# Global filter and MoE on one core: x's first rows through SyncE, a new order of the first batch, Strassen in two chunks more

## The chip, the cores and the metric

The kernel runs on one core of a Trainium2 chip. The metric is device time in microseconds for one launch. Before the change the median of seven runs is 757.11 us (755.1 to 759.68).

The core's engines are TensorE (PE, with PEld for its weight loads), VectorE (DVE), ScalarE (ACT), GpSimd (POOL) and SyncE (SP). In this kernel transfers are issued from SP (queue q1, "hardware dynamic") and from POOL (queue q0, "software dynamic"); only POOL's transfers change fp32 to fp16 on the way.

## What is computed

```python
def _attn_ref(x, filt_r, filt_i):            # x: 8 x 3008 x 256
    X = np.fft.rfft(x, axis=1)
    F = (filt_r + 1j * filt_i)[None, :, :]
    Y = X * F
    y = np.fft.irfft(Y, n=x.shape[1], axis=1)
    return y.astype(np.float32)

def _moe_ref(x, w_in, w_out):                # x: 24064 x 256
    h = x @ w_in                             # 256 x 2048
    g = np.maximum(0.01 * h, h)
    return (g @ w_out).astype(np.float32)    # 2048 x 256
```

The result of the first goes, as 24064 tokens of 256 numbers, into the second.

## The kernel before, in words

**The transform.** A sequence of 3008 is treated as 94 x 32. Stage 1 (s1) is a matrix product over the 94 (`fwd1`), stage 2 (s2) one over the 32 with the twiddle factors in it (`f2`), then comes the product with the filter, then stage 3 (sa, the inverse over 32) and stage 4 (sb, the inverse over 94, matrix `i1`). Between stages 1 and 2, and between 3 and 4, the data must be turned. Stage 4 leaves a batch transposed in `yt`, from which the MoE reads.

**The MoE.** The 24064 tokens form 47 chunks of 512. For each, `moe1` makes h in pairs of 128 rows of w_in (line 501) and ACT turns a pair into g (line 506, leaky ReLU). The second product of a chunk runs while the next chunk's first product does, interleaved matmul by matmul. It is made either in `plain` (line 607: 64 matmuls of 256 columns) or in `products` (line 555): Strassen's scheme in Winograd's form, seven products of 16 matmuls with 128 columns each, over the four quarters of g and of w_out. That needs four sums of quarters of g per chunk (`act_sums`, line 529, VectorE), four sums of w_out once (line 635), and adds that put the products together (lines 579 to 599). The seventh product of a chunk (`last_product`) is made in the slot of the next chunk. Chunks from `W0 = 4` on run so, except the last; chunks 0 to 3 and 46 run in `plain`.

**The first batch.** It is not planned by times but by a list written out by hand, `FIRST`, in which each step is one instruction or a few: s1p (stage 1 on PE), s1e (its copy out of PSUM, A on ACT or D on DVE), t1 (turning, a transpose on VectorE), s2p (stage 2 on PE), s2d (filter product on VectorE from PSUM), s2a and s2m (copy by ACT and filter product on GpSimd), sap and sae (stage 3 and its copy), t2 (second turning), sbp and sbe (stage 4 and its copy), warm (matmuls on zeros), i1 and x (loads of the inverse matrix and of the second batch's x, the latter with w_out between its halves). The engines take their parts of the list in its order. A load whose place must be kept back, such as i1, begins with a small memset on VectorE on the destination, for which the load waits.

Ahead of the list stand the loads: SP issues `small` (fwd1 and the stage 3 matrices) and two thirds of f2; POOL issues x of batch 0 in four parts of 10, 10, 8 and 4 rows, four filter loads, the last third of f2, four filter loads, and w_in. A POOL transfer waits for the eighth before it (the semaphores go round in eight).

**The other batches** are planned by time. The unit is an eighth of a chunk. `PLANS` gives for batches 1 to 3, and for all later ones with a shift of 47 units per batch, where stage 1 begins and its step, the same for stage 2, by how much stage 3 lies behind, begin and step of stage 4, and the place of the x loads of the next batch. Groups are taken one by one, at least `GAP` = 0.6 units apart. The data are turned through DRAM: SP stores stage 1's (line 254) `AFTER[0]` behind the last group, and reads them back (line 261) `LANDED` behind that; stage 3's (lines 324, 268) likewise with `AFTER[4]`. A group of stage 2 or 4 is taken at or behind its read-back's time. In stage 2 the product with the filter needs the two halves of the partitions exchanged: VectorE makes two products (lines 307, 310), SP copies one with its halves exchanged (lines 308, 309) `AFTER[1]` behind, and GpSimd adds (line 313) `AFTER[2]` behind (batch 1: `AFTER[3]`); stage 3 (line 320) needs that sum. Even groups of batch 1 exchange on VectorE (lines 304, 305).

Of the kernel before, what the change touches and what calls it, by code (L numbers as in the profile page):

```python
# [11 lines left out]
P = 128  # L12
# [63 lines left out]
def kernel(  # L76
# [21 lines left out]
    QT = 4 * N1  # L98
    W0 = 4
    GAP = 0.6  # L100
    EXG = 0
    LANDED = 2.25
    SUMS = (0.13, 1.43, 2.87, 3.89)
    REST = (5.89, 12.39, 11.94, 9.93, 24.7, 19.52)
    DUE = (3.46, 1.74)
    TWICE = (1.43, 1.46)
    F2T = 2.82
    LEAD = (3.88, 5.77)
    AFTER = (0.67, 0.83, 2.35, 2.75, 0.3, 0.45)


    PLANS = (
        (0.68, 0.07, 11.58, 1.13, 3.65, 36.62, 2.68, 5.42, 1.67),
        (11.38, 1.67, 43.14, 2.5, 7.25, 86.56, 2.69, 18, 2.16),
        (39.96, 1.81, 76.39, 3.57, 5.42, 129.9, 2.68, -0.73, 2.69),
        (63.95, 2.85, 119.86, 3.87, 7, 177.42, 2.97, 12.93, 2.45),
    )
# [84 lines left out]


    nc.sync.dma_start(small_sb[:], small_d.ap())
    for i in (1, 0):
        nc.sync.dma_start(f2_sb[:, ts(i, NC // FP), :], f2_d.ap()[i])
    first_parts = ((0, 10), (10, 10), (20, 8), (28, 4))
    for n0, nn in first_parts:
        x_load(0, n0, nn)
    for hf in range(2):  # L210

        filt_load(0, filt_r, hf * DH, DH)
        filt_load(64, filt_i, hf * DH, DH)
        if hf == 0:
            nc.gpsimd.dma_start(f2_sb[:, ts(2, NC // FP), :], f2_d.ap()[2])
    nc.gpsimd.dma_start(w_in_sb[:], moe_w_in.rearrange("(dt p) c -> p dt c", p=P))
# [232 lines left out]

    def load_x():  # L450

        x_load(1, 0, N2 // 2)
        nc.gpsimd.dma_start(w_out_sb[:], moe_w_out.rearrange("(ct p) d -> p ct d", p=P))
        x_load(1, N2 // 2, N2 // 2)
        issued.add(("x", 1, 0))

    FIRST = """
        warm 18, s1p 0 0 2 b0, s1e 0 0 2 A, s1p 0 2 4 b3, s1p 0 6 4 b4, s1e 0 2 4 D, warm 4, s1p 0 16 4 b3,
        s1e 0 16 4 D, s1p 0 10 2 b1, s1e 0 6 4 A, s1p 0 12 4 b4, s1e 0 10 2 A, warm 2, s1p 0 24 2 b2,
        s1e 0 12 4 A, s1e 0 24 2 D, s1p 0 20 4 b3, s1e 0 20 4 A, s1p 0 26 2 b0, s1p 0 28 2 b1,  # L460
        s1p 0 30 2 b2, s1e 0 26 2 D, s1e 0 28 2 A, s1e 0 30 2 D, t1 1, t1 0, warm 14, s2p 0 0 4 0 b0,
        s2p 0 0 4 1 b1, s2p 0 16 4 0 b2, t1 2, t1 3, s2a 0 0 4 0, s2m 0 0 4 0, s2a 0 0 4 1, s2p 0 16 4 1 b0,
        s2p 0 8 8 0 b4, s2p 0 8 8 1 b3, s2a 0 16 4 0, s2m 0 16 4 0, s2a 0 16 4 1, s2m 0 16 4 1,
        s2p 0 4 4 0 b1, s2d 0 8 8 0, s2p 0 20 4 1 b2, s2d 0 8 8 1, i1, s2d 0 4 4 0, s2p 0 4 4 1 b0,
        s2p 1 8 8 0 b4, s2d 0 4 4 1, warm 1, s2p 1 8 8 1 b3, s2a 1 8 8 0, s2m 0 0 4 1, sap 0 8 b1,
        s2a 1 12 8 0, s2p 1 16 8 0 b4, s2d 0 20 4 1, sap 0 16 b0, s2m 1 12 8 0, x, s2a 1 8 8 1, s2m 1 8 8 1,
        s2d 1 16 8 0, sae 0 8 A, s2a 1 12 8 1, sae 0 16 A, s2p 0 20 4 0 b2, sap 0 4 b1, s2m 1 12 8 1,
        s2p 1 16 8 1 b3, sap 0 0 b0, s2p 1 0 8 1 b4, s2d 0 20 4 0, s2d 1 16 8 1, sae 0 4 A, s2m 1 8 8 0,
        sae 0 0 A, sap 0 20 b1, s2d 1 0 8 1, sap 0 12 b2, s2p 1 0 8 0 b3, sap 1 16 b0, sae 0 20 A,
        sae 0 12 A, sap 1 12 b1, s2d 1 0 8 0, sap 1 20 b2, t2 0, sap 1 8 b4, t2 1, sae 1 16 A, sap 1 4 b0,  # L470
        sap 1 0 b3, sae 1 12 A, warm 5, sbp 0 1 b1, sae 1 20 A, sae 1 8 A, sbp 0 4 b2, sae 1 4 A, sae 1 0 A,
        t2 3, sbp 0 5 b4, sbe 0 1 A, sbp 0 2 b0, t2 2, sbe 0 4 A, sbp 0 6 b3, sbe 0 5 A, sbp 0 7 b1,
        sbp 0 0 b2, sbp 0 3 b4, sbe 0 6 A, sbp 1 1 b3, sbe 0 0 D, sbe 0 2 A, sbp 1 0 b0, sbe 0 3 A,
        sbe 0 7 A, sbe 1 1 D, sbe 1 0 A
    """
    steps = dict(s1p=s1p, s1e=s1e, t1=t1, s2p=s2p, s2d=s2d, s2a=s2a, s2m=s2m, sap=sap, sae=sae, t2=t2,
                 sbp=sbp, sbe=sbe, i1=load_i1, x=load_x, warm=keep_warm)
    for step in FIRST.split(","):
# [12 lines left out]
    def moe1(ci, ct):  # L491
# [13 lines left out]
        if j == 1:  # L505
# [10 lines left out]
    sums = big[0][:, : 3 * NCH * TH].rearrange("p (i c t) -> p i c t", i=3, c=NCH)  # L516
    s1, s2, s4 = (sums[:, i] for i in range(3))
    part = [big[0][:, 3 * NCH * TH :].bitcast(FP32)[:, ts(i, 2 * TH)].rearrange("p (t k d) -> p t k d", t=2, k=2)
            for i in range(2)]
# [4 lines left out]

    def act_sums(ci, step):
        a11, a12, a21, a22 = (quarter(ci, i, j) for i in range(2) for j in range(2))
        o, i0, i1, op = ((s1, a21, a22, AL.add), (a21, a11, a21, AL.subtract),
                         (s2, s1, a11, AL.subtract), (s4, a12, s2, AL.subtract))[step]
        nc.vector.tensor_tensor(o, i0, i1, op)  # L529
        issued.add(("sum", ci, step))  # L530

    done = {"products": 0}

    def store(ci, tj, of):

        t, end = ci * CH + tj * P, ci * CH + (tj + 1) * P
        lo = 0
        while t < end:
            e = min(end, (t // QT + 1) * QT)
            b, h = divmod(t // QT, N2 // 4)  # L540
            row = b * N + (t % QT) // 4 * N2 + 4 * h
            nc.sync.dma_start(
                bass.AP(tensor=out.tensor, offset=out.offset + row * D,
                        ap=[[N2 * D, (e - t) // 4], [D, 4], [1, D]]), of[lo : lo + e - t])
            lo, t = lo + e - t, e
# [20 lines left out]

    def stores(ci, i):
        for j in range(2):
            store(ci, 2 * i + j, rows(ci, i)[:, j, 0:2, :].rearrange("p k d -> p (k d)"))

# [6 lines left out]
    def last_product(ci):  # L577
        def after(po):
            add(rows(ci, 0)[:, :, 1], po, rows(ci, 1)[:, :, 2], AL.add)
            soon(AFTER[5], lambda: stores(ci, 0))  # L580
        return product(ci, lambda: s4, b22, after, 3)

    def products(ci):
        a11, a12, a21, a22 = (lambda i=i, j=j: quarter(ci, i, j) for i in range(2) for j in range(2))

        def after5(po):
            add(rows(ci, 1)[:, :, 1:3], twice(po), part[1], AL.add)
            soon(AFTER[5], lambda: stores(ci, 1))

        items = product(ci, a11, b11, lambda po: nc.scalar.copy(t1, po))  # L590
        if ci > W0:
            items += last_product(ci - 1)
        else:
            done["products"] += 1
            items += [lambda: None] * (2 * NCH)
        items += product(ci, a12, b21, lambda po: add(rows(ci, 0)[:, :, 0], po, t1, AL.add))
        items += product(ci, a21, wt[2], lambda po: add(v7, po, t1, AL.add), 1)
        items += product(ci, lambda: s2, wt[1], lambda po: add(part[1], twice(po), part[0], AL.add), 2)
        items += product(ci, a22, wt[3], lambda po: add(rows(ci, 1)[:, :, 0], po, u3, AL.add))
        items += product(ci, lambda: s1, wt[0], after5, 0)  # L600
        return items

    def plain(ci):

        def one(tj, ct):
            po = out_banks[(done["products"] + tj) % 2].rearrange("p a t d -> p (a t d)")[:, :D]
            nc.tensor.matmul(po, gts[ci][:, ct, ts(tj, P)], w_out_sb[:, ct, :],  # L607
                             start=(ct == 0), stop=(ct == NCT - 1))
            if ct < NCT - 1:
                return  # L610
            ot = outp.tile([P, D], FP32, tag="ost", padded_shape=[P, 6 * P], name=f"ost_c{ci}_t{tj}")
            (nc.vector.tensor_copy if ci < W0 else nc.scalar.copy)(ot[:], po)
            soon(AFTER[5], lambda: store(ci, tj, ot[:]))
        return [lambda tj=tj, ct=ct: one(tj, ct) for tj in range(4) for ct in range(NCT)]
# [52 lines left out]
    while queue:  # L667
# [4 lines left out]
        else:  # L672
            behind = load_time(stage - 1, b, g // 2) if stage != 1 else 0
        if behind is None or behind + 0.02 > t:
            heapq.heappush(queue, (t + GAP if behind is None else behind + 0.03, n, stage, b, g, f))
# [7 lines left out]
    for ci in range(NCHUNK + 1):  # L683
# [3 lines left out]
        if ci == 0:  # L687
            continue
        wino = W0 <= ci - 1 < NCHUNK - 1
        items = products(ci - 1) if wino else plain(ci - 1)  # L690
        if ci == NCHUNK:
            items = last_product(ci - 2) + items
        for i, f in enumerate(items):
            at(SL * (ci + i / len(items)) + 0.01, f)
        if wino:
            for i in range(4):
                at(SL * ci + SUMS[i], lambda ci=ci, i=i: act_sums(ci - 1, i))
    while work:
# [32 lines left out]
```

## Time and profile before

| what | us |
|---|---|
| median of seven runs | 757.11 |
| the profiled execution, whole | 757.1 |
| its span | 755.1 |
| first MoE matmul (line 501) | 37.63 |
| last MoE matmul's group begins | 742.77 |
| last copy of the output ends | 751.93 |
| granted TensorE clock, mean | 0.997 |

The page of the profile gives busy time per engine, the span in 40 slices, the queues, the chain of waits that ended last, and the costliest groups of instructions. A row names line, engine, operation, output and inputs. From the groups: ACT's leaky ReLU takes 1.02 us for 128x1024, x 376; one sum of `act_sums` 1.25 to 1.30 us for 128x2048, x 168; GpSimd's add 1.38, x 84. From the timeline of the first 38 us: copies of stage 1 take 0.6 (ACT, 512 columns), 1.02 (ACT, 1024), 0.67 and 1.22 (VectorE); a transpose 1.16; a filter product 0.68 (512) or 1.2 (1024) on VectorE and 1.15 (512) on GpSimd.

A time in a list of waits is how long the waiting engine stood idle; one wait for several things is put down to the one that came last. TensorE's matmuls overlap, so that "busy" is not the same as full speed.

### The profile page before, as it was taken

Reading aid. Unit: us, or ns where it says so; the run is one execution under the profiler, and the core shown is the slowest. Engines: PE = TensorE matmul, PEld = TensorE weight load, DVE = VectorE, ACT = ScalarE, POOL = GpSimd, SP = SyncE. Lnnn points to the kernel's source line nnn. Section 1 sums busy time; section 2 is a strip of 40 time slices with the busy share of each in tenths; the row PEclk is TensorE's granted clock in tenths of the full one; section 3 lists DMA queues with packets and bytes.
Section 4 is the critical chain, followed back from the end, with each engine's and each line's share of the span. In section 5 each row is a group of like instructions: output and inputs, shape, how many; then the busy total and the mean of one; then the engine's idle time right before and its main releaser. Section 6 shows DMA issues by size and latency. Waiting matters only on the chain.

```text
span 755.1 us, 19184 instructions
## 1 busy us (share of the span) xinstructions
PE 742.0 (98%) x7920; PEld 529.8 (70%) x7920; DVE 487.5 (65%) x664; ACT 559.8 (74%) x757; POOL 163.7 (22%) x169
## 2 busy tenths in 40 slices
PE   8998999999999999999999999999999999999998
PEld 3655667766777767877778777787777777777776
DVE  5885524777766776576767666676677666555462
ACT  3675787888878777778778777877777777777663
POOL 5503330332132222122223322212111110000000
PEclk9999999999999999999999999999999999999999
DMA  9986788876877567665666656544454433121012
GB/s 190 227 217 154 189 199 226 212 184 179 224 190 169 125 193 189 159 147 148 176 193 161 160 141 190 146 138 128 141 149 129 116 94 102 56 64 53 30 44 70
DMA packets 119688, 113.34 MB, mean 150 GB/s; under 512 B 16352, under 2 KB 92768, under 8 KB 119408
## 3 DMA queue, kind: packets, MB, share of 16 engines
q1 hardware_dynamic: 104736, 95.62, 42.7%
q0 software_dynamic: 14864, 16.49, 15.9%
q8 instruction: 62, 1.02, 0.6%
q14 instruction: 26, 0.21, 0.1%
HBM read 57.51 MB, written 50.33 MB: 143 GB/s over the span
## 4 chain that ended last, share of the span: by engine, by line
PE 91%; DMA 5%; POOL 1%; DVE 1%; SPq 1%; issue 0%; ACT 0%; POOLq 0%; DVEq 0%; ACTq 0%
PE ph L501 41%; PE pf L555 17%; PE po_ps L555 17%; PE pf L249 3%; PE pf L341 3%; PE pf L320 2%; PE pf L298 2%; PE pf L607 2%; PE po_ps L607 2%; DMA p_b_g<-p_b_g 2%; DMA f_sb<-fwd_const 1%; DMA x_sb<-in_x_dram 1%; POOL y_b_g L313 1%; POOL prod L395 1%; DMA big<-dz 1%
## 5 line engine op out<-in xcount | busy, mean ns | idle before, releaser
L506 ACT ACTIVATE gt_c<-ph 128x1024 f16<-128x1024 f32 x376 | 385.0, 1024 | 139.0 <-PE ph L501 126.1
L501 PE MATMUL ph<-yt,w_in_sb 128*128 128x512 f16 (+7 forms) x1728 | 447.5, 351 | 0.4 <-DVE yt L331 0.4
L555 PEld LDWEIGHTS <-gt_c 128*128 128x128 f16 x2688 | 194.8, 98 | 88.4 <-issue 1.3
L313 POOL TENSOR_TENSOR y_b_g<-p_b_g,p_b_g 128x512 f16<-128x512 f32 x84 | 115.6, 1376 | 424.5 <-DMA p_b_g<-p_b_g 255.4
L555 PEld LDWEIGHTS <-big 128*128 128x128 f16 x2016 | 144.1, 98 | 60.9 <-issue 0.6
L501 PEld LDWEIGHTS <-w_in_sb 128*128 128x128 f16 x1728 | 137.6, 98 | 20.5 <-issue 1.7
L307 DVE TENSOR_TENSOR p_b_g<-pf,fb_sb 128x512 f32<-128x512 f32 x78 | 53.8, 689 | 38.1 <-PE pf L298 21.3
L555 PE MATMUL pf<-wt_sb,gt_c 128*128 128x128 f16 x672 | 68.7, 219 | 0.0
L555 PE MATMUL po_ps<-wt_sb,gt_c 128*128 128x128 f16 x672 | 67.7, 219 | 0.1
L252 ACT CAST big<-pf 128x512 f16<-128x512 f32 x100 | 58.4, 584 | 10.1 <-PE pf L249 8.3
L331 ACT CAST yt<-pf 128x376 f16<-128x376 f32 x120 | 56.5, 473 | 11.9 <-PE pf L341 9.6
L555 PE MATMUL pf<-wt_sb,big 128*128 128x128 f16 x672 | 64.5, 219 | 0.0
L555 PE MATMUL po_ps<-w_out_sb,gt_c 128*128 128x128 f16 x672 | 64.4, 219 | 0.0
L555 PE MATMUL po_ps<-wt_sb,big 128*128 128x128 f16 x672 | 64.1, 219 | 0.0
L555 PE MATMUL pf<-w_out_sb,gt_c 128*128 128x128 f16 x672 | 64.0, 219 | 0.0
L310 DVE TENSOR_TENSOR p_b_g<-pf,fa_sb 128x512 f32<-128x512 f32 x84 | 57.3, 682 | 0.3 <-POOL y_b_g L313 0.2
L529 DVE TENSOR_TENSOR gt_c<-gt_c 128x2048 f16<-128x2048 f16 x42 | 54.5, 1297 | 1.0
L322 ACT CAST big<-pf 128x512 f16<-128x512 f32 x84 | 49.0, 583 | 7.3 <-PE pf L320 5.8
L529 DVE TENSOR_TENSOR big<-gt_c 128x2048 f16<-128x2048 f16 x42 | 53.9, 1284 | 0.2 <-ACT gt_c L506 0.2
L529 DVE TENSOR_TENSOR big<-big,gt_c 128x2048 f16<-128x2048 f16 x42 | 52.7, 1255 | 0.0
L529 DVE TENSOR_TENSOR big<-gt_c,big 128x2048 f16<-128x2048 f16 x42 | 52.4, 1248 | 0.0
L607 PEld LDWEIGHTS <-gt_c 128*128 128x128 f16 x320 | 31.1, 98 | 17.7 <-issue 0.5
(87 smaller groups left out, 655.8 us busy)
## 6 DMA issues: line engine op xcount, KB each, us to landing
dz<-big SPq DMA_DIRECT2D x98, 256.0 KB
p_b_g<-p_b_g SPq DMA_DIRECT2D x156, 128.0 KB
out_dram<-ost_c_h SPq DMA_DIRECT2D x114, 128.0 KB
big<-dz SPq DMA_DIRECT2D x42, 256.0 KB
big<-dz SPq DMA_DIRECT2D x56, 192.0 KB
x_sb<-in_x_dram POOLq DMA_DIRECT2D x41, 192.0 KB, 4.5
out_dram<-ost_c_t SPq DMA_DIRECT2D x14, 128.0 KB
x_sb<-in_x_dram POOLq DMA_DIRECT2D x2, 768.0 KB, 10.7
```

Source lines behind the costliest of these rows:

```text
L249: nc.tensor.matmul(ps, fwd1[:N1], x_sb[:N1, ds(2 * g, 2), :], start=True, stop=True)
L252: copy(st[:, ds(2 * (g % 2), 2), :], ps)
L307: nc.vector.tensor_tensor(p2[:], ps, fb, AL.mult)
L310: nc.vector.tensor_tensor(p1[:], ps, fa, AL.mult)
L313: ("y", b, g), lambda: nc.gpsimd.tensor_tensor(y1[:], p1[:], p3[:], AL.add)))
L322: nc.scalar.copy(st2[h % 4][:, ds(2 * (g % 2), 2), :], ps)
L331: copy(yv, ps.rearrange("p c a -> p a c"))
L501: nc.tensor.matmul(ph[:, j, ds(t - ci * CH, e - t)], w_in_sb[:, dt, ts(ct, P)], yt[:, dt, ds(t % N, e - t)], start=(dt == 0), stop=(dt == ...
L506: nc.scalar.activation(gts[ci][:, ds(2 * g, 2), :], ph, AF.Lrelu)
L529: nc.vector.tensor_tensor(o, i0, i1, op)
L555: nc.tensor.matmul(po[:, t], a()[:, c, ts(t, P)], w[:, c, :], start=(c == 0), stop=(c == NCH - 1))
L607: nc.tensor.matmul(po, gts[ci][:, ct, ts(tj, P)], w_out_sb[:, ct, :], start=(ct == 0), stop=(ct == NCT - 1))
```

## The change

x's first six rows per partition are loaded by SP in fp32, into `big1` (free until the first turning), and rounded to fp16 by ACT (four rows) and VectorE (two), the new steps `xc`. The rest of x follows by POOL in three parts; f2's first third stands behind x on POOL, the other two thirds are loaded by SP within the list (step `f2`, with a memset on VectorE). The load of x's second batch and that of w_out are steps of their own: x 0 and x 1 ahead of GpSimd's first filter product, w_out behind its last. The list has a new order.

```diff
+    EARLY = 6
+    x_early = big[1][:].bitcast(FP32)[:, : EARLY * D].rearrange("p (n d) -> p n d", n=EARLY)
     nc.sync.dma_start(small_sb[:], small_d.ap())
-    for i in (1, 0):
-        nc.sync.dma_start(f2_sb[:, ts(i, NC // FP), :], f2_d.ap()[i])
-    first_parts = ((0, 10), (10, 10), (20, 8), (28, 4))
-    for n0, nn in first_parts:
+    nc.sync.dma_start(x_early[:R1], bass.AP(tensor=x.tensor, offset=x.offset, ap=[[N2 * D, R1], [D, EARLY], [1, D]]))
+    for n0, nn in ((6, 10), (16, 10), (26, 6)):
         x_load(0, n0, nn)
+    nc.gpsimd.dma_start(f2_sb[:, : NC // FP, :], f2_d.ap()[0])
...
+    def load_f2():
+        nc.vector.memset(f2_sb[:, NC // FP, 0:2], 0.0)
+        nc.sync.dma_start(f2_sb[:, NC // FP :, :].rearrange("p (i c) m -> p i (c m)", i=FP - 1),
+                          f2_d.ap()[1:].rearrange("i p c m -> p i (c m)"))
+
+    def load_x(half):
+        x_load(1, half * N2 // 2, N2 // 2)
+        issued.add(("x", 1, 0))
+
+    def load_w_out():
         nc.gpsimd.dma_start(w_out_sb[:], moe_w_out.rearrange("(ct p) d -> p ct d", p=P))
...
+    def round_x(n0, n, e):
+        engine[e](x_sb[:N1, ds(n0, n), :], x_early[:N1, ds(n0, n), :])
...
+        xc 0 4 A, xc 4 2 D, warm 18, s1p 0 0 4 b3, s1p 0 4 2 b0, warm 3, s1p 0 14 2 b1, s1e 0 4 2 D,
...
+        s1e 0 6 4 D, s1p 0 16 4 b3, s1e 0 16 4 A, s1p 0 26 2 b2, s1p 0 24 2 b0, s1e 0 24 2 A, f2, s1e 0 20 4 D,
...
+        s2p 0 12 4 1 b4, t1 2, s2d 0 8 4 1, s2p 0 12 4 0 b1, s2p 0 16 8 0 b3, x 0, x 1, s2m 0 0 4 0,
...
+        sap 0 4 b2, i1, s2d 1 0 8 1, sap 0 16 b1, sae 0 12 A, s2p 1 8 8 0 b3, sap 0 20 b0, s2d 1 8 8 1,
...
+        sap 1 12 b1, sae 0 20 A, sap 1 8 b0, s2m 1 16 8 0, sae 1 20 A, s2m 1 16 8 1, w_out, sae 1 12 A,
```

In the planner a group of stage 2 or 4 is taken no earlier than `READ` = 2.2 units behind its read-back, and nearly all constants and plans have new values.

```diff
-    LANDED = 2.25
-    SUMS = (0.13, 1.43, 2.87, 3.89)
+    LANDED = 2.43
+    READ = 2.2
+    SUMS = (0.09, 1.59, 2.35, 4)
...
-    AFTER = (0.67, 0.83, 2.35, 2.75, 0.3, 0.45)
+    AFTER = (0.53, 0.8, 1.33, 3.17, 0.39, 0.52)
...
-        (0.68, 0.07, 11.58, 1.13, 3.65, 36.62, 2.68, 5.42, 1.67),
-        (11.38, 1.67, 43.14, 2.5, 7.25, 86.56, 2.69, 18, 2.16),
-        (39.96, 1.81, 76.39, 3.57, 5.42, 129.9, 2.68, -0.73, 2.69),
-        (63.95, 2.85, 119.86, 3.87, 7, 177.42, 2.97, 12.93, 2.45),
+        (0.68, 0.31, 12.95, 0.9, 4.35, 38.33, 2.78, 7.78, 1.61),
+        (12.19, 1.53, 42.87, 2.62, 7.4, 85.59, 2.85, 16.13, 2.12),
+        (40.7, 1.73, 77.28, 3.57, 5.62, 130.03, 2.65, -0.23, 2.52),
+        (63.95, 2.85, 119.86, 3.87, 7.04, 177.42, 2.92, 12.93, 2.24),
...
             behind = load_time(stage - 1, b, g // 2) if stage != 1 else 0
+            if stage != 1 and behind is not None:
+                behind += READ
```

Strassen covers chunk 3 (`W0` = 3) and the last chunk, 46. The last chunk's sums lie in `big1`, are made partly in halves (`LAST`), and its products follow in the order m1, m7, m2, the s2 product, the a22 product, the s1 product, the s4 product; of its four stores two go by SP's queue and two, one of them in two pieces, by ACT's.

```diff
-    W0 = 4
+    W0 = 3
...
+    last_sums = [v for v in big[1][:].rearrange("p (i c t) -> i p c t", i=4, c=NCH)]
+    LAST = ((-2.9, 1, 0, NCH), (-1.2, 0, 0, NCH // 2), (-0.5, 2, 0, NCH // 2),
+            (1.05, 0, NCH // 2, NCH // 2), (1.1, 2, NCH // 2, NCH // 2), (1.2, 3, 0, NCH // 2), (3.02, 3, NCH // 2, NCH // 2))
...
+        if ci == NCHUNK - 1:
+            items = last_product(ci - 1) + m1() + m7() + m2()
...
+        return items + last_product(ci) if ci == NCHUNK - 1 else items
...
-        wino = W0 <= ci - 1 < NCHUNK - 1
+        wino = W0 <= ci - 1
```

## The prediction

> **What bounds the kernel now.** I read the page first, then TensorE's waits, then the chain of waits at the end and in the first 40 us.
>
> ```profile
> span 755.1 us, 19184 instructions
> ...
> PE 742.0 (98%) x7920; PEld 529.8 (70%) x7920; DVE 487.5 (65%) x664; ACT 559.8 (74%) x757; POOL 163.7 (22%) x169
> ```
>
> TensorE is the bound: 13 us of the span are not PE-busy. What PE waits for from 36 us to the end (engine, line, releaser: total us, times, longest):
>
> ```profile
> PE pf L298 <- DMA big<-dz: 2.9, 1, 2.9
> PE pf L320 <- POOL y_b_g L313: 1.5, 2, 1.0
> ```
>
> So once the MoE runs (first L501 matmul at 37.63), only some 5 us can be won by ordering; the rest must come from fewer matmul columns, an earlier 37.63, or a shorter tail. The tail (start, us, what):
>
> ```profile
> 743.59 0.89 PE pf L555 x16
> 744.49 1.80 PE po_ps L607 x16
> 746.28 1.75 PE pf L607 x16
> 748.03 1.75 PE po_ps L607 x16
> 749.78 1.76 PE pf L607 x16
> 751.54 0.02 issue
> 751.56 0.37 ACT ost_c_t L612
> ```
>
> A plain chunk costs 1.80+1.75+1.75+1.76 = 7.06 us, a Strassen product 0.89, hence seven 6.23. The start:
>
> ```profile
> 1.25 6.56 DMA x_sb<-in_x_dram
> ...
> 8.09 10.81 DMA f_sb<-fwd_const
> ...
> 26.02 0.59 POOL x_sb L190
> 26.62 1.17 POOL w_out_sb L453
> 27.79 0.53 POOL x_sb L190
> ...
> 28.32 3.40 POOL prod L395 x3
> ```
>
> Three things hold it: x's landing, the third part of f2 (landing 18.9), and 2.3 us of DMA issues between GpSimd's products.
>
> **The change, part by part.**
>
> *Strassen for chunk 3.* 7.06 - 6.23 = **-0.8 us** of PE time on the path. Its four sums (1.25 us each, row L529) and adds fall on a VectorE with 2.6 us of work in 97 to 112 us: covered.
>
> *Strassen for the last chunk.* PE saves the same 0.8. Walking VectorE's new order from 743.6: last chunk's gelu rows end at 744.26 (ACT); two half sums of s1 and s2 at about 0.65 each, a half of s4, then the add of m7, due at 746.3, ends at 747.3, while the matmuls that need its bank could start at 747.0: 0.35 late; the next bank 0.2 late. PE ends at 743.43 + 8 x 0.89 + 0.55 = 751.1, the last add (0.17 after, 0.42 long, as L579) at 751.7, beside ACT's copy at 751.93 now. The stores then come three at once, two of them one behind the other on ACT's queue (0.55 us per issue, row L542): the last issue ends at 752.9, now 752.6. Bounds -0.8 to +1.0; I take **0**.
>
> *Read-backs ahead of use (READ).* By the planner, batch 1's last s1 group is at 0.68 + 15 x 0.6 = 9.68 units, its read-back at 9.68+0.67+2.25 = 12.60, the first user at 12.63. New: read-back at 9.68+0.53+2.43 = 12.64, user at 12.64+2.2+0.03 = 14.87. Unit here: (58.73-37.63)/12.60 = 1.67 us. So the user comes 3.7 us after the issue, where it took 4.04 (58.73 to 62.77, 3.90 of it the DMA). Of the 2.92 us wait 0.3 stays: **-2.6**. The MoE matmuls that fill it are there in any case.
>
> *Planner numbers.* y waits: both fall in batch 3, where stage 3 follows stage 2 by 5.42 units, new 5.62; at (743.4-37.6)/376 = 1.88 us a unit each wait shrinks by 0.4: **-0.7** (bounds -1.5, +1.5: the same two exchange DMAs still queue behind four read-backs on SP). The y-add also moves up in GpSimd's queue (2.35 to 1.33 units behind), where it blocks the x loads behind it; those have 20 units and more in the later batches. The exception is batch 2's first x load: from 7.77 to 10.07 units, its user from 11.38 to 12.19, so 2.1 units, 3.5 us, for a load of median 4.5 (min 2.7): 0 to +1, I take **+0.5**.
>
> *First stage.* x's first six rows go by SyncE in fp32, f2 behind. The 18 warm-up matmuls still end at 7.8, so the first s1 matmul stays at 7.8 if rounding (ACT 128x1024: 1.02, by row L506) is done; it would be 1 us late only if that load landed at 7.8 as x's does now, and it has 576 KB in place of 960. The last x, now 13.1, comes sooner by what 512 KB of f2 take among it (2.6 us at the 198 GB/s of 10 to 20 us; some of it ran before x's first packet: I take 1.5), but eviction takes over: VectorE has 4 x 0.67 + 2 x 1.22 of copies from 8.5 on, with waits for banks; the transposes start at 14.4 (now 14.76). They take 4.6, to 19.0. With f2 in time the ten filter products (4 x 0.68 + 6 x 1.2 = 9.9) run 19.0 to 28.9, now 20.39 to 30.9. GpSimd issues x ahead of its first product and w_out behind its last: eight products of 1.15 end at 28 (now 31.7). Second transposes and last stage as now: MoE at 35.4, **-2.2**, if the inverse matrix i1 is there by 31.2.
>
> *i1.* Its memset now follows the sixth product on VectorE: 24.1 in place of 22.7; its SP issue can't be earlier. And x's second batch, two halves of 3.7 us each (w_out landed at 38.5, 11.9 after its issue, the second half behind it at 42.2, 14.4 after its own), is in GpSimd's DMA queue at 17 to 18 us, ahead of it, not at 26. What that means, in the DMA queue view (queue: packets, MB, share) of 23.2 to 26.0, 26.0 to 29.3 and 106.1 to 108.9:
>
> ```profile
> q0 software_dynamic: 145, 0.59, 105.4%
> ...
> q1 hardware_dynamic: 144, 0.77, 56.4%
> ...
> q0 software_dynamic: 214, 0.39, 100.4%
> ```
>
> i1 was issued at 22.80 and SP's queue (q1) moved nothing till 26.0: GpSimd's w_in had all 16 engines. Again at 106: an SP store waits while 214 packets, 13 per engine, of four x loads go. The Trainium skill, "DMA: Bandwidth & Descriptors", section "Queues, rings and completion order", says otherwise: each engine takes turns between the queues packet by packet. By the rule i1 would need its own 1.9 us (56.4% of 3.3) and about twice that of turns from 24.9 on, landing near 30.5: no wait, MoE 35.4. By the row it stands behind w_in (issued 15.49, 12.6 to land: 28.1) and one or both x halves (31.8, 35.5), landing 33.7 to 37.3. The rows decide; I take 34.2. From the first L432 to the first L501 it is 34.23 to 37.63, 3.4 us, now; so MoE at 37.6: **0**, bounds -2.2 and +3.1.
>
> *f2's other two thirds* go the same way: SP issues them at about 11.5, with the filter loads ahead in GpSimd's queue. Taking turns they need twice the 1.5 us that I gave them ahead of x, so 15.5 with the latency; behind all filters (the last issued at 14.35, median 9.7 to land) 24 at most, while the third s2 group wants them at 17.7. The filters' rows are short (256 bytes each) and SP comes in the middle of them, so I take in time; at 22 the MoE would come at 39.8, +2.2, inside i1's bounds.
>
> *Clock.* Columns: us, then PE, PEld, DVE, ACT, POOL busy, granted clock, DMA share, GB/s:
>
> ```profile
> 16.60:20.00 3.40, 1.97 (x32) 1.31 (x30) 2.78 (x3) 1.68 (x4) 1.15 (x1) 1.00 1.69 208
> 20.00:23.40 3.40, 3.40 (x47) 2.68 (x45) 3.01 (x5) 0.47 (x1) 3.34 (x3) 0.51 1.46 211
> ```
>
> After a stretch with 1.97 of 3.40 us busy the clock was halved. The skill, "TensorE: Matmul & The Clock Gate", Part 1, asks a whole idle window for that; by it the new order, about as busy there, keeps its clock and the s2 matmuls gain 0.9 us. By the row it drops again. I take the row, 0; with i1 late it would not count.
>
> **Sum**: -0.8 + 0 - 2.6 - 0.7 + 0.5 + 0 = -3.6. The profiled execution took 757.1 (755.1 and 2 around it), the median of the seven is 757.11: **753.5 us**.
>
> **Rivals.**
> - *B, start-up whole*: i1 by 31.2, MoE at 35.4: 751.3. For it: the rule on turns, and the shorter packets ahead of i1. Against: the 2.9 us of silence.
> - *C, i1 behind both x halves*: lands 37.3, MoE at 40.7, +3.1: 756.6. For: four loads were drained at 106. Against: SP started there with part of them left.
> - *D, the other side: i1 behind w_out too*, issued at 28 while i1 still waits. w_out takes 5.5 us (33.0 to 38.5 in landings): i1 at 42.8, MoE at 46.2, +8.6: 762.1. It decides from an i1 later than 39.3. Against: no SP DMA waited longer than 3.4 us in the trace.
> - *E, the read-back wait is only moved*: batch 1 gets 2.2 units later, so its last stages press on their due times; 2.6 not won: 756.1. Against: by the planner the least distance to a due time in batch 1 is still 0.9 units, 1.5 us (now 1.7 units), and batch 4 runs with 0.9 now without a wait.
>
> **Numbers.** A 0.45 (own range 752 to 755.5), B 0.20, C 0.17, E 0.10, D 0.08. Faster by over 0.2% (1.5 us, what a measurement of this kernel can tell): A, B and a third of C and E, 0.73; within: 0.15; slower: D and a rest of C and E, 0.12. Range 750.5 to 757: B's lower side, C's centre; D stays out.
>
> **What would show it.** First L501 at 35.4 (B), 37.6 (A), 40.7 (C); a wait of L432's TensorE for the i1 load; no L298 wait on big<-dz over 0.5; L320 waits under 1 in sum; L607 down from five chunks to three, L555 up by two times seven products; PE end near the same distance of 3.5 us from the span's end. I am wrong if the MoE starts beyond 39 or if new waits of over 2 us stand in TensorE's list after 120 us.

## The result, and the profile after

After the change the median is 756.64 us (27 runs, 755.49 to 758.72); the kernel before, run again beside it, has 756.65 us (64 runs, 753.99 to 759.89). The ratio is 1.0002, its 95% interval 0.9992 to 1.0011: no difference. The forecast was 753.5 us.

The profiled execution took 756.03 us, 1.07 less than the one of before. That one lay 0.45 above its median, this one 0.6 below: this explains the distance between the profiles and the medians, and the sum below is made between the two profiled executions.

The page (span, then busy time, share and instructions per engine):

```profile
span 754.2 us, 19393 instructions
...
PE 739.9 (98%) x8017; PEld 529.6 (70%) x8017; DVE 502.2 (67%) x686; ACT 559.5 (74%) x755; POOL 165.6 (22%) x168
```

TensorE has 2.1 us of busy time less, the span only 0.9: the difference became idle time. TensorE's waits from 34.5 us to the end (what waits, for what: us in total, times, longest):

```profile
PE pf L433 <- DMA i_sb<-inv_const: 3.9, 1, 3.9
PE pf L299 <- DVE p_b_g L311: 1.0, 1, 1.0
PE pf L250 <- DVE big L253: 0.9, 2, 0.5
PE pf L321 <- DVE p_b_g L311: 0.4, 1, 0.4
```

The wait for the read-back (big<-dz, 2.9) and those for y (1.5) are gone. New at the top stands one of 3.9 us: line 433 is stage 4's product of the first batch (432 before), and what it waits for is i1. The chain of waits through the first 40 us (start, us, what):

```profile
11.52 6.86 DMA f_sb<-fwd_const
...
24.43 10.52 DMA i_sb<-inv_const
...
38.56 1.88 PE ph L511 x4
```

f2's rest is issued at 11.52 and in at 18.38 (its last part before the change: 18.90). i1 is issued at 24.43 and in at 34.95, 10.52 us later. TensorE had ended stage 3 at 30.3 and its four matmuls on zeros at 31.2; stage 4 and the first MoE matmul, 38.56, follow from i1. GpSimd's filter products end at 27.1 (31.7 before), VectorE's at 29.1 (30.9): the new order has what it needs for an earlier start, and i1 alone holds it back.

The chain at the end:

```profile
741.21 0.91 PE po_ps L575 x16
...
744.88 1.05 PE po_ps L575 x16
745.93 0.93 PE pf L575 x16
746.87 0.90 PE po_ps L575 x16
747.77 0.91 PE pf L575 x16
748.67 0.02 issue
748.70 0.42 DVE ost_c_h L600
```

The last chunk runs as eight groups of 16 matmuls (its seven products and the last of chunk 45). One of them, at 744.88, begins some 0.2 us late, behind VectorE's add that ends at 744.84; the other VectorE rows left out between 742 and 745 lie beside products on other banks. TensorE is done at 748.67, but the span ends at 754.24, 5.57 us later. Before, it was 3.60 (751.54 to 755.14). The store issues in the last six microseconds (line, queue, count: shortest/median/longest in ns, first and last start):

```profile
L562 ACTq DMA_DIRECT2D out_dram<-ost_c_h x3: 692/922/1219, 748.5 to 750.6; - x3
L562 SPq DMA_DIRECT2D out_dram<-ost_c_h x2: 540/544/549, 748.5 to 749.2; - x2
```

ScalarE has three issues in a row, and the last of them, 120 of the 128 KB of one output tile, starts at 750.6, 1.5 us behind the end of the add that made it (749.12). The same tile before the change, in two pieces on SyncE (749.5 to 751.3 us):

```profile
L542 SPq DMA_DIRECT2D out_dram<-ost_c_t x2: 697/804/910, 749.6 to 750.3; - x2
```

| stretch of the profiled execution | before | after | difference | forecast |
|---|---|---|---|---|
| to the first MoE matmul | 37.63 | 38.56 | +0.93 | 0 |
| from there to chunk 45's last product | 705.96 | 702.65 | -3.31 | -3.6 |
| from there to TensorE's end | 7.95 | 7.46 | -0.49 | -0.4 |
| from there to the span's end | 3.60 | 5.57 | +1.97 | +0.4 |
| span | 755.14 | 754.24 | -0.90 | -3.6 |

The main stage won nearly what was forecast; the first stage and the last stores gave 2.9 us of it back. That accounts for 2.7 of the 3.6 us that are missing. The other 0.9 is the distance between this pair of profiled executions, which differ by 1.07 us, and the medians, which do not differ; the timed runs of the two kernels spread over 3 and 6 us.

### The profile page after: what moved, and what is told of

It is laid out like the page before. It is cut to its first block, busy times and chain, and to the rows that moved or that the text cites. A ratio compares the mean times of both kernels' runs of the same rounds, so it can differ in the third digit from the quotient of the medians.

```text
span 754.2 us, 19393 instructions
## 1 busy us (share of the span) xinstructions
PE 739.9 (98%) x8017; PEld 529.6 (70%) x8017; DVE 502.2 (67%) x686; ACT 559.5 (74%) x755; POOL 165.6 (22%) x168
## 4 chain that ended last, share of the span: by engine, by line
PE 92%; DMA 4%; DVE 2%; POOL 1%; ACT 0%; issue 0%; SPq 0%; DVEq 0%; POOLq 0%
PE ph L511 42%; PE po_ps L575 18%; PE pf L575 18%; PE pf L250 3%; PE pf L342 3%; PE pf L321 2%; PE pf L299 2%; DMA i_sb<-inv_const 1%; DMA p_b_g<-p_b_g 1%; PE po_ps L636 1%; PE pf L636 1%; PE po_ps L364 1%; DMA f_sb<-fwd_const 1%; POOL y_b_g L314 1%; PE pf L433 0%; DVE big L253 0%
## 5 line engine op out<-in xcount | busy, mean ns | idle before, releaser
L575 PEld LDWEIGHTS <-gt_c 128*128 128x128 f16 x2800 | 202.2, 98 | 91.3 <-issue 0.2
L575 PEld LDWEIGHTS <-big 128*128 128x128 f16 x2128 | 151.3, 98 | 61.6 <-issue 0.2
L575 PE MATMUL pf<-w_out_sb,gt_c 128*128 128x128 f16 x720 | 67.9, 219 | 0.0
L575 PE MATMUL po_ps<-wt_sb,big 128*128 128x128 f16 x720 | 67.4, 219 | 0.0
L575 PE MATMUL pf<-wt_sb,big 128*128 128x128 f16 x704 | 67.2, 219 | 0.0
L548 DVE TENSOR_TENSOR gt_c<-gt_c 128x2048 f16<-128x2048 f16 x43 | 57.3, 1332 | 1.0
L548 DVE TENSOR_TENSOR big<-big,gt_c 128x2048 f16<-128x2048 f16 (+1 forms) x45 | 56.0, 1245 | 0.1
L548 DVE TENSOR_TENSOR big<-gt_c 128x2048 f16<-128x2048 f16 (+1 forms) x46 | 55.9, 1214 | 0.1
L548 DVE TENSOR_TENSOR big<-gt_c,big 128x2048 f16<-128x2048 f16 (+1 forms) x45 | 53.6, 1192 | 0.0
L250 PE MATMUL pf<-x_sb,small_sb 94*128 94x512 f16 x112 | 42.8, 382 | 0.9 <-DVE big L253 0.9
```

The lines of the kernel that those rows point to most:

```text
L250: nc.tensor.matmul(ps, fwd1[:N1], x_sb[:N1, ds(2 * g, 2), :], start=True, stop=True)
L548: nc.vector.tensor_tensor(*(v[:, ds(c0, n)] for v in (o, i0, i1)), op)
L575: nc.tensor.matmul(po[:, t], a()[:, c, ts(t, P)], w[:, c, :], start=(c == 0), stop=(c == NCH - 1))
```

## The experiments

Theory: two separate losses eat the gain, i1 that lands too late at the start and the stores at the end. Rivals: the start is late for another reason; the end takes its time whatever the queue; the gain in the main stage is no gain. The table has the stretches of each profiled execution, the median of the timed runs, and the ratio to the kernel before with its 95% interval. "Start" is the first MoE matmul, "main" runs from there to chunk 45's last product, "end" from there to the end of the span. The experiments ran in three sets on different chips (e1 to e4, e5 to e8, e9 to e12), and the kernel before, run with each set, had medians of 756.67, 757.02 and 757.30 us: across sets the ratio compares better than the medians do.

| kernel | start | main | end | median us | ratio to before |
|---|---|---|---|---|---|
| before | 37.63 | 705.96 | 11.55 | 756.65 | 1 |
| after | 38.56 | 702.65 | 13.03 | 756.64 | 1.0002 (0.9992 to 1.0011) |
| e1 | 35.65 | 701.77 | 13.01 | 753.28 | 0.9952 (0.9940 to 0.9964) |
| e2 | 34.56 | 702.11 | 13.04 | 751.70 | 0.9931 (0.9918 to 0.9943) |
| e3 | 38.83 | 702.40 | 12.98 | 756.02 | 0.9985 (0.9974 to 0.9996) |
| e4 | 38.91 | 703.04 | 12.15 | 755.60 | 0.9985 (0.9975 to 0.9996) |
| e5 | 34.34 | 702.30 | 12.15 | 750.62 | 0.9908 (0.9887 to 0.9929) |
| e6 | 38.93 | 702.65 | 11.49 | 755.03 | 0.9982 (0.9970 to 0.9993) |
| e7 | 38.32 | 703.34 | 12.99 | 757.49 | 1.0005 (0.9991 to 1.0018) |
| e8 | 39.22 | 709.66 | 13.32 | 762.44 | 1.0069 (1.0043 to 1.0094) |
| e9 | 40.14 | 703.73 | 13.01 | 757.47 | 1.0002 (0.9986 to 1.0019) |
| e10 | 34.25 | 702.53 | 13.01 | 751.78 | 0.9921 (0.9890 to 0.9952) |
| e11 | 34.34 | 702.94 | 11.49 | 750.15 | 0.9902 (0.9874 to 0.9931) |
| e12 | 34.80 | 702.56 | 11.94 | 751.09 | 0.9912 (0.9883 to 0.9941) |

### The start: where i1 stands among the transfers (e1, e2, e3, e10)

e1 issues i1 right behind f2:

```diff
-        s1e 0 6 4 D, s1p 0 16 4 b3, s1e 0 16 4 A, s1p 0 26 2 b2, s1p 0 24 2 b0, s1e 0 24 2 A, f2, s1e 0 20 4 D,
+        s1e 0 6 4 D, s1p 0 16 4 b3, s1e 0 16 4 A, s1p 0 26 2 b2, s1p 0 24 2 b0, s1e 0 24 2 A, f2, i1, s1e 0 20 4 D,
...
-        sap 0 4 b2, i1, s2d 1 0 8 1, sap 0 16 b1, sae 0 12 A, s2p 1 8 8 0 b3, sap 0 20 b0, s2d 1 8 8 1,
+        sap 0 4 b2, s2d 1 0 8 1, sap 0 16 b1, sae 0 12 A, s2p 1 8 8 0 b3, sap 0 20 b0, s2d 1 8 8 1,
```

> The changed kernel with the inverse matrices (i1) issued by SyncE directly behind the rest of f2, at about 12 us, so ahead of the two x halves of the next batch. Theory (late matrices): with i1 landed by about 23 nothing but the work itself sets stage 4; TensorE no longer idles 3.9 us, its clock is not halved at 33.6, and the first MoE product starts at 35.4 to 36.0 instead of 38.56; the time falls by 2.5 to 3.2 us, to about 753.8. Rival (only moved): 752 KB go ahead of the second half of the filter and of w_in while the DMA engines are full; products of stage 2 then wait for fa, the first MoE product comes at 37 to 40, and the time is within 1 us of the changed kernel's 756.6.

The start came at 35.65, no wait for i1 was left, the clock stayed full, and the median lies 3.4 us below the changed kernel's. A little of the rival is true as well: the filter's rows of 256 bytes were in at 24.9 instead of 21.9, and the chain of waits runs through a filter load (in at 25.30).

e2 puts i1 between the filter and the x halves, and these behind GpSimd's first product:

```diff
-        s2p 0 12 4 1 b4, t1 2, s2d 0 8 4 1, s2p 0 12 4 0 b1, s2p 0 16 8 0 b3, x 0, x 1, s2m 0 0 4 0,
+        s2p 0 12 4 1 b4, t1 2, s2d 0 8 4 1, i1, s2p 0 12 4 0 b1, s2p 0 16 8 0 b3, s2m 0 0 4 0, x 0, x 1,
...
-        sap 0 4 b2, i1, s2d 1 0 8 1, sap 0 16 b1, sae 0 12 A, s2p 1 8 8 0 b3, sap 0 20 b0, s2d 1 8 8 1,
+        sap 0 4 b2, s2d 1 0 8 1, sap 0 16 b1, sae 0 12 A, s2p 1 8 8 0 b3, sap 0 20 b0, s2d 1 8 8 1,
```

> The changed kernel with i1 issued behind the product s2d 0 8 4 1 on VectorE (about 19 us instead of 24.5) and the two x halves behind GpSimd's first product (about 19 us instead of 14.8). Theory (late matrices): i1 needs 7 to 10.5 us from its issue, so it lands at 26 to 29.5, before TensorE's need at 31.2; first MoE product at 35.4 to 36.0, time about 753.8 to 754.5, with up to 1 us given back where the first s1 group of batch 1 waits for an x half that lands at 36 or later. Rival (the DMA engines are full until 35 whatever the order, so that something of the start is late anyway): the wait moves to x, 1 to 3 us, and the time stays at 756 to 757.

The start came at 34.56, sooner than expected, the median lies 4.9 us lower, and no wait for x appeared although its last packet ended at 36.9. So there was room in the DMA engines; it was the order that was wrong. Whether it was i1's late issue or the transfers beside it, e1 and e2 can't say: they changed both. e3 was to leave the issue and move only the x halves:

```diff
-        s2p 0 12 4 1 b4, t1 2, s2d 0 8 4 1, s2p 0 12 4 0 b1, s2p 0 16 8 0 b3, x 0, x 1, s2m 0 0 4 0,
+        s2p 0 12 4 1 b4, t1 2, s2d 0 8 4 1, s2p 0 12 4 0 b1, s2p 0 16 8 0 b3, s2m 0 0 4 0,
...
-        sap 0 4 b2, i1, s2d 1 0 8 1, sap 0 16 b1, sae 0 12 A, s2p 1 8 8 0 b3, sap 0 20 b0, s2d 1 8 8 1,
+        sap 0 4 b2, i1, x 0, x 1, s2d 1 0 8 1, sap 0 16 b1, sae 0 12 A, s2p 1 8 8 0 b3, sap 0 20 b0, s2d 1 8 8 1,
```

> The changed kernel with i1 where it is (issued at about 24.4) and the two x halves moved behind it in GpSimd's order, as they stood before the change. Theory (it is the x halves already queued that make i1 take 10.5 us): i1 lands within 7 to 8 us, at 31.5 to 32.5, first MoE product at 35.6 to 36.5; the x halves land at 36 to 40, and the first s1 groups of batch 1 wait 0 to 3 us; time 754.5 to 757. Rival (i1 is late because it is issued late, the queue ahead of it does not matter): i1 still lands at 34 to 35, first MoE product at 38 to 38.6, and the time is 756.6 or up to 2 us above.

That test missed its aim. GpSimd, ahead of VectorE in the list at that point, issued the x halves at 23.8 and 24.4, i1 came between them at 24.1, and it landed 11.1 us later. In the profiled execution it made no difference that the x halves were handed over at 23.8 instead of 14.8: their first packet came at 26.2 instead of 26.1, as w_in's packets, which are ahead in GpSimd's queue, were ending. But six of e3's 22 timed runs took 752.7 to 754.9 us, less than any of the 27 of the changed kernel (from 755.5), and its interval lies below 1. No such run was profiled; what happens in them is open. e10 moves them behind GpSimd's last product:

```diff
-        sap 1 12 b1, sae 0 20 A, sap 1 8 b0, s2m 1 16 8 0, sae 1 20 A, s2m 1 16 8 1, w_out, sae 1 12 A,
+        sap 1 12 b1, sae 0 20 A, sap 1 8 b0, s2m 1 16 8 0, sae 1 20 A, s2m 1 16 8 1, x 0, x 1, w_out, sae 1 12 A,
```

> The changed kernel with i1 where it is (issued at about 24.4) and the x halves behind GpSimd's last product, at about 27, so that their packets no longer lie beside those of i1 (in e3 GpSimd reached them at 24.0, still ahead of i1). Theory (i1's packets are stretched by the x halves beside them: 6.1 us from first to last packet against 3.1 us in the kernel before): the wait for i1 falls by 2 to 3 us, i1 in at 31 to 32, first MoE product at 35.6 to 36.2; the x halves land at 38 to 40 and the first s1 group of batch 1 waits for them 1 to 3 us; time 754 to 756. Rival (i1 is late by its issue alone): wait of 3 us or more, first MoE product at 38 or later, and the wait for x on top: 757 to 759.

i1 was issued at 24.0, in the changed kernel at 24.4, and the whole loss was gone: start at 34.25, median 751.78, both better than expected. The DMA queues of the changed kernel from 28 to 34 us (queue: packets, MB, share of the 16 engines' time):

```profile
q0 software_dynamic: 128, 0.92, 73.0%
q1 hardware_dynamic: 125, 0.75, 31.3%
```

and of e10 from 26 to 29.6 us:

```profile
q1 hardware_dynamic: 144, 0.77, 51.5%
q0 software_dynamic: 54, 0.23, 46.0%
```

In the changed kernel i1 (q1, 128 packets of 6 KB) and the x halves (q0, packets of 8 KB) go nearly one for one (112 of the 128 packets of q0 carry data), and i1 needs 6.1 us from its first packet to its last (27.9 to 34.0). With the x halves behind it, it begins 1.9 us sooner and needs 3.4 (26.0 to 29.4); in the kernel before it was 3.1 (26.0 to 29.1).

Why i1's first packet comes so late is a question of its own. In the changed kernel and the one before, it comes about when w_in's packets end, as if i1 stood behind w_in. e2 shows that it need not: issued there at 19.62, i1 has its first packet at 23.24, with w_in's packets still going. The queues of e2 from 19.7 to 23.2, where q1 has no row, and from 23.3 to 27.3 us:

```profile
q0 software_dynamic: 1412, 0.71, 149.1%
...
q0 software_dynamic: 113, 0.46, 57.1%
q1 hardware_dynamic: 124, 0.75, 47.3%
```

i1 waits 3.6 us and then takes turns with w_in. What sets this delay (3.5 us in the changed kernel, 2.0 in e10) was not found.

What sets e10's start is the work itself, in the chain of waits:

```profile
26.30 0.92 DVE prod L396
...
28.65 2.29 DVE big L425 x2
30.94 0.04 issue
30.98 0.46 PE pf L433 x8
31.44 0.02 issue
31.47 2.74 ACT yt L332 x7
34.21 0.04 issue
34.25 0.38 PE ph L511
```

VectorE's last filter product, the second turning, stage 4, ScalarE's copies, and the MoE, with no transfer in it. The x halves end at 37.8 and nobody waits for them.

### The clock in the wait (e9)

e9 fills TensorE's wait with 18 more matmuls on zeros:

```diff
-        sae 1 8 A, sap 1 16 b3, sae 1 16 A, sap 1 4 b2, t2 1, sae 1 4 A, sap 1 0 b4, t2 0, sae 1 0 A, warm 4,
+        sae 1 8 A, sap 1 16 b3, sae 1 16 A, sap 1 4 b2, t2 1, sae 1 4 A, sap 1 0 b4, t2 0, sae 1 0 A, warm 22,
```

> The changed kernel with 18 products more whose result is thrown away, in TensorE's wait for i1 (22 instead of 4 before the first product that reads it). They compute nothing of the output. Theory (the idle 3.9 us halve the clock from 33.6 to 40.5, which stretches stage 4 and the first MoE products): i1 still lands at 34 to 35, but the clock stays full; the first MoE product at 37.9 to 38.3 instead of 38.56, its first four matmuls take 1.06 us instead of 1.88; 1.0 to 1.5 us in all, time 755.3. Rival (stage 4 runs at the pace of its evictions on ScalarE, not of TensorE's clock): 756.4 or more.

The clock in the changed kernel (columns: stretch in us, its length, then PE, PEld, DVE, ACT, POOL busy with counts, granted clock, DMA share, GB/s):

```profile
26.80:30.22 3.42, 3.42 (x23) 1.63 (x22) 3.42 (x4) 2.94 (x7) 1.49 (x2) 1.00 1.06 262
30.22:33.63 3.41, 0.99 (x5) 0.26 (x3) 3.41 (x4) 1.09 (x3) 0.00 (x0) 1.00 0.98 270
33.63:37.05 3.42, 1.96 (x51) 1.99 (x53) 0.54 (x2) 1.37 (x4) 0.00 (x0) 0.50 1.16 198
37.05:40.46 3.41, 3.29 (x41) 1.95 (x37) 0.64 (x2) 1.89 (x5) 0.00 (x0) 0.50 1.46 200
```

and in e9:

```profile
31.69:35.10 3.41, 3.03 (x15) 1.18 (x12) 1.65 (x2) 0.00 (x0) 0.00 (x0) 1.00 1.05 252
35.10:38.51 3.41, 1.63 (x54) 1.66 (x56) 0.43 (x1) 1.15 (x4) 0.00 (x0) 1.00 1.27 185
38.51:41.93 3.42, 3.11 (x42) 1.95 (x38) 0.96 (x3) 2.46 (x7) 0.00 (x0) 1.00 1.13 153
```

The clock did stay full, the first four MoE matmuls took 1.18 us instead of 1.88, and from i1's landing to the first of them it was 3.4 us instead of 3.6. That is 0.9 us (0.7 and 0.2). But in e9's profiled execution i1 landed 12.69 us after its issue, at 36.75, where six other kernels with i1 beside the x halves (the changed kernel, e3, e4, e6, e7, e8) have it at 34.7 to 35.6; and the ratio shows no gain. So the half clock costs about 0.9 us inside the loss, and filling the wait did not make the kernel faster. Whether the added products had a part in i1's later landing was not tried.

### The end (e4, e6, e12)

e4 gives the two pieces of the cut store to two queues:

```diff
-            queue.dma_start(
+            (queue if e == end else nc.scalar if ci == NCHUNK - 1 else queue).dma_start(
...
-                  nc.scalar if ci == NCHUNK - 1 and j else nc.sync)
+                  nc.scalar if ci == NCHUNK - 1 and j and i else nc.sync)
```

> The changed kernel with the store of the output tile that is cut in two pieces (8 KB and 120 KB) spread over both queues at the end: 8 KB by ScalarE's queue, 120 KB by SyncE's; in the changed kernel both stood behind each other in ScalarE's queue, issued at 749.36 and 750.62, while the last add ended at 749.12. Theory (the end is set by three issues in a row of 0.7, 1.2 and 0.9 us on ScalarE): the last issue starts at about 749.8 and its data land at about 752.1 instead of 753.25; from TensorE's end to the end of the span 4.4 us instead of 5.5; time 755.5. Rival (the 512 KB written at the end take their time whatever the queue): still 5.2 to 5.6 us, time 756.6.

As expected: 1.0 us less in the median. (That alone would not show it, since e3, with the end unchanged, has the same ratio; the trace does, and so does e5's.) From TensorE's end (749.42) to the span's end 4.68 us, 0.9 less than in the changed kernel. Its store issues:

```profile
L562 SPq DMA_DIRECT2D out_dram<-ost_c_h x3: 539/548/880, 749.3 to 750.5; - x3
L562 ACTq DMA_DIRECT2D out_dram<-ost_c_h x2: 698/946/1194, 749.3 to 750.1; - x2
```

The last issue starts 1.1 us behind TensorE's end; in the changed kernel it was 1.9. SyncE issues 128 KB in 0.54 us, ScalarE the same in 0.70, and its piece of 8 KB, which came second, in 1.19.

e6 takes Strassen's products out of the last chunk alone and gives it the copies and stores of before:

```diff
-        wino = W0 <= ci - 1
+        wino = W0 <= ci - 1 < NCHUNK - 1
         items = products(ci - 1) if wino else plain(ci - 1)
+        if ci == NCHUNK:
+            items = last_product(ci - 2) + items
...
-            nc.vector.tensor_copy(ot[:], po)
+            (nc.vector.tensor_copy if ci < W0 else nc.scalar.copy)(ot[:], po)
```

> The changed kernel with the last chunk multiplied out plainly again, with its stores as before the change; chunk 3 stays with Strassen's products. Theory (the last chunk's Strassen saves 14 products of 0.055 us, and its two late 256 KB of stores cost more): from the start of chunk 45's last product to the end of the span 11.5 us as before instead of 13.0, time 755.2. Rival (the longer end belongs to this one profile, the last chunk's Strassen is worth its 0.8 us): time 757.4.

The median fell to 755.03. Its chain at the end:

```profile
741.58 0.89 PE po_ps L575 x16
...
747.76 1.76 PE po_ps L636 x16
749.52 0.02 issue
749.54 0.37 ACT ost_c_t L641
```

7.94 us of TensorE from chunk 45's last product on instead of 7.46, but then only 3.55 to the end of the span (753.07) instead of 5.57. In the plain form one tile of the output is done every 1.75 us and its store goes out beside the next; in Strassen's form everything that is stored is done in the last microsecond. The 0.5 us saved on TensorE cost 2.0 behind it. (The expectation's count of 14 products is off: plain is 128 matmuls' worth of 128 columns, Strassen's seven products are 112, so 16 are saved.)

e12, which exchanges the two pieces of e5's cut store, won nothing:

```diff
-            queue.dma_start(
+            (nc.scalar if e == end and ci == NCHUNK - 1 and tj == 1 else queue).dma_start(
```

> e5 with the two pieces of the cut store exchanged: the 120 KB by ScalarE's queue right behind its first store, the 8 KB last by SyncE's. Theory (the last large issue sets the end): the 120 KB are issued at about 0.65 us behind TensorE's end instead of 1.15, the end comes 0.3 to 0.5 us sooner, 4.2 us behind TensorE's end instead of 4.7, time 750.2. Rival (an issue on ScalarE takes 0.7 to 1.2 us against 0.55 on SyncE, so that nothing is won): 750.6 to 751.0.

Its end is 0.2 us shorter, the start of its run 0.5 later, the median 0.5 above e5's. The 120 KB now took ScalarE 1.44 us to issue. That is the rival's reason, but the sizes lie within the scatter, and the test is inconclusive.

### The main stage (e7, e8)

e7 makes chunk 3 plain again:

```diff
-    W0 = 3
+    W0 = 4
```

> The changed kernel with chunk 3 plain again. Theory (14 products of 128x256 at 0.055 us each less per chunk on a TensorE that is the bound): 0.8 us slower, 757.4, with the stretch from the first MoE product to chunk 45's last product at 703.4 instead of 702.65. Rival (chunk 3 falls in a stretch where TensorE waits anyway, or the sums on VectorE make the evictions of other groups late): no difference, 756.6.

The main stage has 703.34, 0.7 above the changed kernel, and the median lies 0.85 above. Both fit the 0.8 us, but neither shows it: the ten kernels whose edits leave the main stage alone (e1 to e6, e9 to e12) have 701.77 to 703.73 there, and against the kernel before, run with each, the ratios are 1.0005 and 1.0002. What chunk 3's products are worth in time stays open.

e8 gives the planner its old numbers (cut here):

```diff
-    LANDED = 2.43
-    READ = 2.2
-    SUMS = (0.09, 1.59, 2.35, 4)
...
+    LANDED = 2.25
+    READ = 0
+    SUMS = (0.13, 1.43, 2.87, 3.89)
...
```

> The changed kernel with all of the planner's numbers as before the change and READ at 0 (the read-backs are again issued without the 2.2 us ahead of their use); the first stage, chunk 3 and the last chunk stay as changed. Theory (the wait of 2.9 us for the read-back in batch 1 and about 0.7 us of waits for y went with the new numbers): the waits are back, the stretch from the first MoE product to chunk 45's last product is 705 to 706 instead of 702.65, time 759 to 760. Rival (the waits were only a shift: without them the same time is lost elsewhere in the main stage): within 0.7 us of the changed kernel.

The direction was right, the expected size too small: the median lies 5.8 us above the changed kernel's, 5.1 by the ratios. TensorE's waits of e8:

```profile
PE pf L433 <- DMA i_sb<-inv_const: 4.3, 1, 4.3
PE pf L342 <- DMA big<-dz: 3.0, 1, 3.0
PE pf L299 <- DMA big<-dz: 3.0, 1, 3.0
```

The wait of batch 1 is back (line 299), and a second read-back is late too (line 342, stage 4), which the kernel before did not have. Around the first:

```profile
61.71:65.13 3.42, 0.69 (x5) 0.18 (x3) 0.55 (x1) 1.02 (x1) 0.00 (x0) 0.98 0.80 212
65.13:68.54 3.41, 3.15 (x14) 1.94 (x15) 2.25 (x4) 0.00 (x0) 0.28 (x1) 0.51 0.35 134
```

the idle stretch also halved the clock for 3.4 us. Two waits of 3.0 us and half of 3.4 add up to some 7.7, about the 7.0 us by which the main stage is longer than in the changed kernel. The new numbers do remove these waits, and the time does not come back elsewhere. Why the old numbers leave two waits in the new kernel and one in the old was not followed.

### Both repairs together (e5, e11)

e5 has the edits of e2 and e4, e11 those of e2 and e6.

> Both repairs in one kernel: i1 issued ahead of the x halves (as in e2, 751.7 us) and the cut store spread over both queues (as in e4, 1.0 us below the changed kernel). Theory (two separate losses, one at each end of the span): they add up, 750.6 us, first MoE product at 34.5, from TensorE's end to the span's end 4.4 us. Rival (the two are not independent, or e2's gain was partly the luck of a run): 751.5 or more.

> i1 ahead of the x halves (as in e2) and the last chunk plain with its old end (as in e6). Theory (the gains of the two add up): 751.7 less the 1.6 us that e6 lies below the changed kernel, so 750.1; from the start of chunk 45's last product to the span's end 11.5 us. Rival (the last chunk's products with the spread stores of e5 are as good or better): 750.6 or more.

Both came out as the sum of their parts, 750.62 and 750.15. Neither waits for i1, and the half clock at the start is gone. They are about 0.9 to 1.0% faster than the kernel before, and 6.0 and 6.5 us below the changed kernel's median; between the two the intervals do not decide.

## Why the prediction was wrong, by its own steps

- **i1, the first step that failed.** "The rows decide; I take 34.2", so MoE at 37.6 and a change of 0. i1 landed at 34.95, 0.75 later; from there to the first MoE matmul it took 3.6 us instead of 3.4, under the halved clock; the start came out at +0.93. The mechanism was wrong beyond the number. The text let i1 stand behind w_in and one or both x halves, because SyncE's queue had moved nothing for 3.2 us, and dropped the Trainium skill's rule ("DMA: Bandwidth & Descriptors", section "Queues, rings and completion order": each DMA engine takes turns between its queues, packet by packet). In the trace i1's first packet comes 3.5 us after its issue (24.43 to 27.91), a delay that e2 has with w_in still moving, and from 28 to 34 us it takes turns with the x halves, 112 data packets of theirs against 125 of its own, much as the rule says. The rule alone missed as well: its 30.5 let the turns begin at 24.9. That 34.2 was nearly met is in part luck; i1 did not stand in the line that it was worked out from.
- **Rival B**, start-up whole, was given 751.3 us with a start at 35.4. e2 and e10 have 751.7 and 751.8, but with starts at 34.6 and 34.3, and the end's +1.5 on top: that the sum agrees is chance. The -2.2 us that the new order was credited with are there and more (by e10 -3.4), but not in the kernel as it is: the x halves ahead of i1 took them.
- **The last chunk, the second step that failed, and the larger.** "The last issue ends at 752.9, now 752.6", bounds to +1.0, taken at 0. TensorE's part was right: 7.46 us, forecast 7.5. From the end of the last add to the end of the last issue the text had 1.2 us, two issues of 0.55 each; it was 2.4 (749.12 to 751.50): 0.2 until ScalarE was free, then 1.22 and 0.92 for the two pieces of the cut tile. This is most of the +1.5 that the whole end measured, beyond the bound of +1.0. The price of 0.55 is that of a whole tile. The cut tile had cost 0.70 and 0.91 on SyncE in the profile before. The text's own sign, TensorE's end 3.5 us from the span's end, came out at 5.6. Without the change (e6) the median is 1.6 us lower.
- **READ and planner numbers.** -2.6, -0.7 and +0.5, with chunk 3's -0.8: the main stage fell by 3.31 of the 3.6, and about 0.7 of its 702.65 are the half clock on the first MoE matmuls. e8 confirms READ and the planner's numbers together by undoing them; the share of chunk 3 is not confirmed. Rival E, a wait only moved, falls; what is left at line 299 is a new wait of 1.0 us, for VectorE.
- **f2's two thirds** came at 18.4, behind the 17.7 at which they were wanted; TensorE waited 0.4: nearly right. **Batch 2's first x load**, entered at +0.5, showed no wait.
- **The clock** at 20 us was expected to drop as in the row. It did not: TensorE was busy for 2.83 of the 3.41 us from 16.57 to 19.98, not 1.97; at this place the rule that the text had set against the row came out right. It dropped in the wait for i1 instead.
- **Rivals C and D**: i1 took turns with the x halves and did not stand behind them, and w_out (first packet at 35.3) came after it.

So the two terms entered at 0, i1 and the last chunk, both with bounds that reached above 0, came out at +0.93 and +1.5: the first from a wrong picture of the queues, the second from a price for a store issue that did not hold for a cut tile on ScalarE.

## What to carry to other kernels

When loads share the DMA engines at the start, rank them by when their first reader needs them: a transfer issued early for a later stage took every second turn here from one that was needed next, and moving 1.5 MB behind 0.75 MB was worth 4.9 us (e10) without any load becoming late. At the end of a kernel count from TensorE's last matmul to the end of the last store: a form that saves products but completes all of its outputs together can lose more in stores than it saved. A cost entered at zero between bounds of both signs deserves a price read from the same piece of work on the same queue.

## What the runs showed of the hardware that was not expected

- A store issue on ScalarE cost 0.69 us for 128 KB in 128 rows (SyncE 0.54), and 1.19 to 1.22 us for a piece of 8 KB that came second (SyncE, before the change: 0.70). From the end of the last store issue to the end of the span it was 2.4 to 2.7 us in all fourteen kernels, so the end moved with the last issue.
- i1's first packet came 2.0 to 3.7 us after its issue in all kernels but e1 (5.3, with f2's rest ahead of it on its own queue). All had GpSimd's loads going.
- The clock did not follow the busy time of a stretch alone. After 1.96 of 3.42 us busy (33.63 to 37.05 of the changed kernel) it stayed at half for another stretch; after 1.63 of 3.41 us (e9, 35.10 to 38.51) it stayed full. The Trainium skill ("TensorE: Matmul & The Clock Gate", Part 1) ties the drop to a whole idle window of about 3.4 us; here it came after a window with 0.99 of 3.41 us busy, TensorE having stood idle for the last 2.4 us, and the measurement decides. How the chip counts was not settled.
- After the same kind of wait for i1 the half clock lasted 3.4 us in e3, e6 and e7 and 6.8 us in the changed kernel, e4 and e8; the first four MoE matmuls then took 1.2 or 1.9 us.
